# The 1e-9 of the early softmax sums moved from ScalarE to VectorE, with a new order of operations, in a fused attention and gated-MLP kernel

## The chip, the cores and the metric

The kernel runs on one core of one Trainium2 chip. The metric is the time that the device takes for one execution, in microseconds (us). The engines of the core are TensorE (PE in the rows; PEld is its weight load), VectorE (DVE), ScalarE (ACT), GpSimd (POOL) and SyncE (SP), which here only issues DMA transfers. TensorE writes its products into PSUM, which has eight banks of 512 float32 columns; VectorE and ScalarE read them from there.

## What is computed

Causal attention with a bias from cumulative sums, for 8 batches of 8 heads, 576 positions and 64 columns a head, and then a gated MLP on the heads laid side by side:

```python
scores = scale * q @ k.T + min(-(cum[:, None] - cum[None, :]), 0)   # causal
attn = exp(scores - max); attn = attn / (sum(attn) + 1e-09)
x = attn @ v                                  # 8 heads make 512 columns
h = gelu(x @ w_in); u, v = h[..., :512], h[..., 512:]
v_n = (v - mean) / sqrt(var + 1e-06) * g_ln
v_s = w_sg @ v_n + b_sg                       # mixes the 576 positions
out = x + (u * v_s) @ w_out
```

## The kernel before

**Tiles.** A head's 576 rows of scores are cut into five row tiles `it` (64, 128, 128, 128 and 128 rows). For each tile TensorE makes the scores in a bank of the pair `pss` (or, for the 64 rows in the early pass, of `psm`). VectorE adds the mask, writes the tile to `p` and takes the row minimum `mn` (function `ttr`, the `ISA` rows of VectorE: the second of a pair only reads out `mn`). ScalarE takes the exponential with its row sum (`exp_`, sums in `few`). Then `norm` adds 1e-9 to the sums of the head, takes the reciprocal `rs` and multiplies the tiles by it, on an engine that a table names. TensorE transposes the tiles through `psp` (`turned`), an engine copies them to `pT`, TensorE multiplies by `v` (`sums_of`), and two heads together make one tile `xr` of `x`.

**The first batch.** Heads 0 to 7 go in two passes, with operands in full float32: pass a (`scores_a`, `context_a`) makes row tiles 0, 1 and 2, which need only the first 320 keys, and pass b (`scores_b`, `context_b`) makes tiles 3 and 4. The softmax sums of a head in pass a are therefore three columns wide (`rs` 128x3), in pass b two, and from head 8 on five. The buffers of p rotate over three slots (two of `p`, one named `e`). From head 8 on the operands are split into a high and a low part (`kh`, `kl`).

**The MLP.** For each batch there are five v units (xs times the v half of `wi`, then GELU and layer norm on VectorE, ScalarE and GpSimd), eight u units, eight s units (`ws` times `vn`) and eight o units (`wo` times `gt`, added to `xr` and stored). The banks `psm` carry them. The weights `w_in` and `w_out` come in as 64-bit numbers (`pair`) and are turned into two float32 parts with three wide VectorE operations, a ScalarE read and two splitting steps (`wh`, `wl`) for each 128x512 piece. The scratch for that is a bank of `psm`, too.

**Filling work.** 49 matmuls of `wt` into one bank (nine at the start, 40 more in the order) compute nothing that is used. The first v unit writes into that same bank (`psm_63`), so all 49 come ahead of it.

**What sets the order.** Nothing is issued as the code is written. `Plan` collects all 6791 operations with what they depend on. `order` runs a list scheduling with written-out costs (`cost`) and waits (`LAT`) back and forth `ROUNDS` times, and then once more with an offset for every operation from the table `SHIFT`. What comes out is the sequence that every engine gets, and each engine works through its own sequence in order: an instruction that waits holds up all behind it on its engine. The tables `ENG` and `ALT` name, for each kind of step, which engine takes its first, second, third ... occurrence (s ScalarE, g GpSimd, v VectorE): `na` and `nb` are the multiplications by `rs` in the two passes, `ea`, `eb`, `eb1` the copies of transposed tiles, `wh` and `wl` the weight splits, `xva` and `xvb` the copies to `xr`, `xa` and `xal` the splits of `xr`, `n` and `ev` the same for later heads.

```python
res = self.forward(lat, [p + 200.0 * float(x) for p, x in zip(prio, shift)])
...
nc.scalar.activation(out=rs[:, c], in_=sums[pslot(h)][:, c], func=AF.Copy, bias=1e-9)
nc.vector.reciprocal(out=rs[:, c], in_=rs[:, c])
```

Almost all instructions are recorded through one helper, so the rows carry one line number, L441 before (L450 after); they are told apart by the tiles.

Of the kernel before, what the change touches and what calls it, by code (L numbers as in the profile page):

```python
# [23 lines left out]
DH = DFF // 2  # L24
# [45 lines left out]
    "na": "sggggsssgsggsvvsggggvgggsgsgvgvg",  # L70
    "wh": "sssvvggssggg",
    "ea": "ssvsssss",
    "xva": "v",
    "xa": "gvsgsvss",
    "xal": "gv",
    "nb": "gggsvsggggssvggsggv",
    "eb1": "ssvsvsvv",
    "xvb": "ssss",
    "rt": "gvgggv",
    "vl": "gv",  # L80
    "kh": "ssssssssgg",
    "kl": "gggggggvggv",
    "wsh": "sssssssgsvsg",
    "wsl": "gggvgggvgggg",
    "n": "ggggggggggggggggggggggggsggvgsvgggvvvsgsggvvvvsggvsgsgggsv",
    "ev": "svsvssssvsssvssv",
    "ev1": "svsvsvs",
    "xv": "vv",
    "xw": "s",
    "xz": "ss",  # L90
    "gh": "vsvsssv",
    "gl": "vvgggvv",
    "xh": "ss",
# [12 lines left out]
    "c-n2-dHk1C`akf~uAO!jB~g|vS&M90!`KyO>^oz|)-<bO44-JBQfZM&DygJWQM4<iec#ijMSIeEzRz>`&0jzF<K5@|zVEYK%j<ew*E#1_B9sl~{y$ggust"  # L106
    "4#U&giZowzC%3B|+D@#lDr)-hfmdd4TiqhVt_Gkg+jgb-%MD&f2Macma;s^8A|Vptk$hBHHv@b~az{8KnTTpd=$isAR+weU~(?g%%AW}#kq+`ngs7sB;=J"
    "sZ}?E5j3>w+^Qpr%h<5<?G=e`TBi$+4nc{^>TQY9P8p(^WPT!7W&7n@r=+YoD!Z34Z^>|ym&ZP2o1ydI4qV6l|ls)mN#3I&?Qv!yiwR2{~I0&{|)~RSB9V"
    "BzIaR66ibK2ac&$QKZ+gW^7wq%5+}!bF_5^1PlK>Ez8=mZ$#dbs@J)O<d>G$|7aDz1>>IBm-|s@r&^QdyzeB7O7RH5fe|#g{;M>eNFiwcm<2P|kd@WuZ>S"
    "%X3{xv)u&SRG+!@*cTlnQr+=Hb$CVmOWF<KvRJNc+Jt#(LyhA3u%#V^dbDV5VEcpTnypIWBaL{|ejU{o!3wy-Ks!LkT0jqQzaIPwYjm4{7sbtZdZ7v1+*7"  # L110
    "$hE_@Y<IHR`ot4xvLFt~qhA!tg!yFM8cz(@X@5&NAyoFfQ1~_;jAcVrHavkh55;Biig0dt+xJ)5@C~yTgjS(S7#us%_)&IFKEBVrfAa0kX8K(i$oqA}^X~"
    "49Z_?qM@TTXlkonE<UOd9?)8b`(`F3~_*4D-sJUgF`e=|eVa7-Aa#d~BO9;d_}aa8Qi`tP|0#IEsupMmj1S2tGf9zSrWr+>T0-m$H#yB;6LL0S)Sr<-rxJ"
    "na@+#xC()GIw`<s!z9ADU6Ee(zjT+h+UV)S?+zW)y()xe2l%O^Xfd;1U~KpCDlV3VN3kZxSiuy#&|#e5(`7;wD<)7T+7EBMM%GRoWFxa#%2*!AzTuc#dR4"
    "IW1zS-o4qE6USjX_!c=k8gM5ABq<EJ;e-Ia6(lAN-fhRrKV4ya0;^!i(Z(Kvy&&aSXj*KU<{Teci;lmE`3tC^u*S+YplI=c^d&s;w?xoc@mP<DHI&OfolH"
    "n_34ir!QwC+ZqnRMUe{?zzZ_#W~~hnsRlJ`1BeXgf6?Ys{AM9=cWudtmFFupxdDXXA>QBp=S3z1e#RN&Argt@wL-ti=;Au*yG-Q<!c3&E8|&T?1c#G2iXs"
    "kNp3tYbwm09V%-1CbsEF>$z;+fu}ZLm)fBvJ^P97qj5K%G{RVuVY(RnccNuG*XMC1U51L{VeH(AwIk1Mi%01_m6Qwg+#T!E?!2%h?qHQC!-9<Cmtne+Sl_"
    "1Kd&Za(e~Kew7nq;NwtLyS5!PtOLe)Yc^Uf6W?_hzC<AeP8FSczM-sh7+>~N4&=h3)II61t95&DJ$@G&Ajt>x2Zy9EE;6z&hl(&sjOcp^TzM66znwHC$KX"
# [427 lines left out]
def tile_attn_gmlp(  # L545
# [114 lines left out]
    def pslot(h):  # L660
        return h % (3 if h < N3 else 2)
# [789 lines left out]
```

## Time and profile before

| | |
|---|---|
| time, median of two runs | 737.61 us (736.52 and 738.69) |
| the profiled execution | 737.75 us, of which 736.0 us from first to last instruction |
| TensorE busy | 726.3 us, 99% of the span |
| VectorE, ScalarE, GpSimd busy | 483.4, 482.8 and 526.0 us |
| TensorE's granted clock | full speed, mean 0.999 |
| DMA | 88.35 MB, mean 120 GB/s |

A busy share is the time in which an engine has at least one instruction in flight. The shares are means over stages that differ much: the first 120 us build up the pipeline, then follows a long steady part. A row of a timeline gives the start, the time until the last of its instructions ends, engine, operation, and in square brackets how long the engine had been idle before and what ended that.

### The profile page before, as it was taken

How to read it: one execution, taken by the hardware profiler on the slowest of the kernel's cores; microseconds unless marked ns; L12 is line 12 of the kernel's file. 1: busy time of each engine (PE TensorE's matmuls, PEld its weight loads, DVE VectorE, ACT ScalarE, POOL GpSimd, SP SyncE). 2: the span in 40 equal slices, each digit the busy share in tenths (PEclk: the TensorE clock that was granted, in tenths of full speed). 3: DMA queues.
4: the chain of work that ended last, by engine and by line, in shares of the span. 5: the costliest groups of instructions: out<-in, count | busy, mean ns of one | idle time of the engine just before them, and what ended most of it. 6: DMA issues, size and time to landing. Idle time of an engine off the chain costs nothing.

```text
span 736.0 us, 16276 instructions
## 1 busy us (share of the span) xinstructions
PE 726.3 (99%) x5337; PEld 640.8 (87%) x5337; DVE 483.4 (66%) x1524; ACT 482.8 (66%) x1306; POOL 526.0 (71%) x941
## 2 busy tenths in 40 slices
PE   8999999999999999999999999999999999999998
PEld 6876879988899888998889898998889988899998
DVE  6799977777775567646684477746667456844552
ACT  4988986687885667756676568746777457742341
POOL 5775989749779686886858868687775967873532
PEclk9999999999999999999999999999999999999999
DMA  8893744655455443434534444435544354200101
GB/s 210 252 234 102 199 125 121 169 141 149 128 135 133 130 115 104 124 110 124 147 86 119 123 125 127 106 92 144 132 108 119 95 135 114 61 9 34 47 9 64
DMA packets 59272, 88.35 MB, mean 120 GB/s; under 512 B 16306, under 2 KB 33972, under 8 KB 59188
## 3 DMA queue, kind: packets, MB, share of 16 engines
q1 hardware_dynamic: 59188, 87.32, 44.5%
q8 instruction: 42, 0.69, 0.4%
q14 instruction: 42, 0.34, 0.2%
HBM read 41.37 MB, written 9.73 MB: 69 GB/s over the span
## 4 chain that ended last, share of the span: by engine, by line
PE 91%; DVE 3%; DMA 2%; POOL 2%; ACT 1%; issue 1%; SPq 1%; ACTq 0%; DVEq 0%; POOLq 0%
PE psm L441 54%; PE psp L441 21%; PE pss L441 15%; DMA pair<-in_w_in 1%; DVE p L441 1%; SPq L441 1%; DVE psm L441 1%; POOL p L441 0%; DMA raw<-in_kq 0%; POOL wi L441 0%; POOL rt L441 0%; ACT p L441 0%; DVE gt L441 0%; DVE vt L441 0%; DVE u L441 0%
## 5 line engine op out<-in xcount | busy, mean ns | idle before, releaser
L441 POOL TENSOR_SCALAR p<-p,rs 64x64 f32<-64x64 f32 (+4 forms) x396 | 177.8, 458 | 55.9 <-DVE rs L441 37.8
L441 ACT ACTIVATE p<-p,mn 64x64 f32<-64x64 f32 (+4 forms) x310 | 172.5, 558 | 57.4 <-DVE mn L441 55.7
L441 DVE CUSTOM_DVE_ANT_0 p<-pss,mask 128x448 f32<-128x448 f32 (+4 forms) x304 | 121.0, 425 | 37.0 <-PE pss L441 27.7
L441 PE MATMUL psm<-gt,wo 128*128 128x288 f32 x720 | 125.0, 299 | 0.0
L441 PE MATMUL pss<-k,q 128*128 128x288 f32 (+9 forms) x672 | 122.2, 297 | 0.2
L441 PE MATMUL psm<-xs,wi 128*128 128x288 f32 x720 | 119.3, 300 | 0.0
L441 PE MATMUL psm<-ws,vn 128*128 128x288 f32 x708 | 114.1, 297 | 0.0
L441 PEld LDWEIGHTS pss<-k,q 66*128 66x128 f32 (+3 forms) x672 | 102.2, 180 | 9.3 <-DVE mn L441 0.5
L441 POOL TENSOR_TENSOR k<-raw,k 128x576 fp32r<-128x576 f32 x54 | 77.3, 1431 | 44.8 <-ACT k L441 41.1
L441 PE MATMUL psm<-wi,xs 128*128 128x512 f32 (+1 forms) x380 | 106.6, 401 | 1.0 <-DVE gt L441 1.0
L441 PEld LDWEIGHTS psm<-gt,wo 128*128 128x128 f32 x720 | 105.3, 188 | 1.7
L441 PEld LDWEIGHTS psm<-xs,wi 128*128 128x128 f32 x720 | 102.6, 188 | 2.4 <-issue 0.4
L441 PEld LDWEIGHTS psm<-ws,vn 128*128 128x128 f32 x708 | 100.2, 188 | 0.9 <-DVE vt L441 0.3
L441 PE MATMUL psp<-pT,vf 128*64 128x64 f32 (+3 forms) x752 | 90.1, 387 | 0.0
L441 PEld LDWEIGHTS psp<-pT,vf 128*64 128x64 f32 x752 | 46.9, 137 | 43.9 <-issue 32.1
L441 PEld LDWEIGHTS psm<-wi,xs 128*128 128x128 f32 (+1 forms) x380 | 66.3, 184 | 13.2 <-DVE gt L441 1.2
L441 ACT COPY pT<-psp 128x512 f32<-128x512 f32 x130 | 72.0, 581 | 8.7 <-PE psp L441 8.1
L441 PE MATMUL psp<-ident,p 128*128 128x128 f32 x744 | 72.3, 247 | 0.3 <-POOL p L441 0.3
L441 PEld LDWEIGHTS psp<-ident,p 128*128 128x128 f32 x744 | 69.7, 140 | 3.0 <-POOL p L441 0.5
L441 DVE SCALAR_TENSOR_TENSOR u<-u,psm 128x288 f32<-128x288 f32 x120 | 52.7, 445 | 18.6 <-ACT u L441 18.2
L441 POOL TENSOR_TENSOR gt<-u,gt 128x288 fp32r<-128x288 f32 (+1 forms) x62 | 49.6, 804 | 18.7 <-ACT gt L441 18.2
L441 ACT ACTIVATION_READ_ACCUMULATOR p<-p,mn 128x1 f32 (+1 forms) x310 | 58.5, 189 | 0.0
(157 smaller groups left out, 1105.2 us busy)
## 6 DMA issues: line engine op xcount, KB each, us to landing
q<-k SPq DMA_DIRECT2D x168, 144.0 KB
raw<-in_kq SPq DMA_DIRECT2D x56, 288.0 KB
vf<-in_vp SPq DMA_DIRECT2D x56, 192.0 KB
out_t<-u SPq DMA_DIRECT2D x64, 144.0 KB
k<-k SPq DMA_DIRECT2D x56, 144.0 KB
pair<-in_w_in SPq DMA_DIRECT2D x8, 512.0 KB
u<-xs SPq DMA_DIRECT2D x32, 64.0 KB
pair<-in_w_out SPq DMA_DIRECT2D x4, 512.0 KB
```

The lines of the kernel that those rows point to most:

```text
L441: fn(*args, **kw)
```

## The change

There are two parts. In `norm`, for the heads of the first batch (`SPL` is 8) and the call that holds row tile 0, which is the call of pass a, the addition of 1e-9 is a VectorE `tensor_scalar` on 128x3 elements in place of a ScalarE activation. That is eight instructions. Pass b and all later heads keep the ScalarE form.

```diff
     def norm(h, its, rs):
         c = slice(min(its), max(its) + 1)
-        nc.scalar.activation(out=rs[:, c], in_=sums[pslot(h)][:, c], func=AF.Copy, bias=1e-9)
+        if h < SPL and 0 in its:
+            nc.vector.tensor_scalar(out=rs[:, c], in0=sums[pslot(h)][:, c], scalar1=1e-9, scalar2=None, op0=ALU.add)
+        else:
+            nc.scalar.activation(out=rs[:, c], in_=sums[pslot(h)][:, c], func=AF.Copy, bias=1e-9)
         nc.vector.reciprocal(out=rs[:, c], in_=rs[:, c])
```

The other part is the tables. `SHIFT` has new numbers for nearly all operations, in steps of 50 instead of 200, and `ALT` names other engines for some occurrences. Two lines of it as examples:

```diff
-    "na": "sggggsssgsggsvvsggggvgggsgsgvgvg",
+    "na": "sgsgvsgvvvsvsgvsgvgsvgsgsgssssgv",
-    "ea": "ssvsssss",
+    "ea": "ssssvvvs",
-            res = self.forward(lat, [p + 200.0 * float(x) for p, x in zip(prio, shift)])
+            res = self.forward(lat, [p + 50.0 * float(x) for p, x in zip(prio, shift)])
```

The operations and their dependencies are the same; the sequences of the engines change from the first rows to the last. In the late part an instruction moves by some ten places among thousands. In the first 120 us engines change too. Counted in the sequences up to the end of the fifth piece of `w_in` (`gt_133`), VectorE gets in the new kernel the eight additions, two more copies to `pT`, one more copy to `xr` (128x320), four more multiplications by `rs` (128x320, 128x128, two of 64x64) and one more low part of `wi` (128x512). It gives up two casts (`wi` 128x512, `xs` 128x320) and one subtraction (`xs` 128x320). GpSimd has eight multiplications by `rs` and one `wi` part less there, and two `xs` steps more. ScalarE has the eight additions, one multiplication and one copy less, and three multiplications and one cast more.

Three places are shown as they stand in the sequences.

**The start.** SyncE's first transfers before (`in_ka` are the queries and keys of pass a: `kq_80`, `kq_81`, `kq_82` of heads 0, 1, 2, `arena` of the later ones; `in_va` the values):

```order
L441 DMA xs_76<-in_s_t 64x576
L441 DMA kq_80<-in_ka 64x640
L441 DMA kq_82<-in_ka 64x640
L441 DMA pair_105<-in_w_in 128x1024
L441 DMA kq_81<-in_ka 64x640
L441 DMA e_71<-in_va 128x512
L441 DMA pair_121<-in_w_in 128x1024
L441 DMA arena_79<-in_ka 64x1280
L441 DMA pair_112<-in_w_in 128x1024
```

and now:

```order
L450 DMA xs_76<-in_s_t 64x576
L450 DMA kq_80<-in_ka 64x640
L450 DMA pair_105<-in_w_in 128x1024
L450 DMA kq_81<-in_ka 64x640
L450 DMA e_71<-in_va 128x512
L450 DMA pair_121<-in_w_in 128x1024
L450 DMA e_71<-in_va 128x512
L450 DMA kq_82<-in_ka 64x640
L450 DMA pair_112<-in_w_in 128x1024
L450 DMA vf_147<-in_vp 128x320
L450 DMA arena_79<-in_ka 64x1280
```

The keys of head 2 (`kq_82`) moved from the third place to the eighth, those of head 1 from the fifth to the fourth, and those of heads 3 and 4 (`arena`, 64x1280) from the eighth to the eleventh. TensorE's sequence for the same stretch, before (`sel` matmuls add the cumulative sums):

```order
L441 MATMUL psm_63<-wt_77 128x512 x12
L441 MATMUL pss_58<-kq_80 128x320
L441 MATMUL pss_58<-kq_80 128x192
L441 MATMUL psm_63<-wt_77 128x512
L441 MATMUL psm_64<-kq_80 128x64
L441 MATMUL psm_63<-wt_77 128x512 x2
L441 MATMUL pss_59<-kq_81 128x320
L441 MATMUL pss_59<-kq_81 128x192
L441 MATMUL pss_59<-xs_86,sel_88 128x192
L441 MATMUL pss_59<-xs_86,sel_88 128x320
L441 MATMUL psm_64<-xs_86,sel_88 128x64
```

and now:

```order
L450 MATMUL psm_63<-wt_77 128x512 x16
L450 MATMUL pss_59<-kq_81 128x320
L450 MATMUL pss_59<-kq_81 128x192
L450 MATMUL psm_63<-wt_77 128x512
L450 MATMUL pss_58<-kq_80 128x320
L450 MATMUL pss_58<-kq_80 128x192
L450 MATMUL pss_59<-xs_86,sel_88 128x192
L450 MATMUL pss_59<-xs_86,sel_88 128x320
L450 MATMUL psm_64<-kq_80 128x64
L450 MATMUL psm_64<-xs_86,sel_88 128x64
```

Head 1 now comes ahead of head 0, sixteen filling matmuls stand in front of it in place of twelve, and no others between but one. Ahead of the first scores from `arena_79` (head 3) there are 34 filling matmuls now, and 26 before.

**Pass a on VectorE**, around the reciprocals of heads 0 and 1 (`rs_104`, `rs_108`; the `e_71` and `mn_109` rows are the masks of head 2), before:

```order
L441 MEMSET q_0_25_97 2x576
L441 MEMSET vnr_30_102 2x512
L441 RECIPROCAL rs_104<-rs_104 128x3
L441 ISA e_71,mn_109<-pss_58,mask_18_90 128x320
L441 ISA mn_109 128x1
L441 RECIPROCAL rs_108<-rs_108 128x3
L441 ISA e_71,mn_109<-pss_58,mask_89 128x192
L441 ISA mn_109 128x1
L441 TENSOR_SCALAR psm_64<-psm_64 128x512
```

and now:

```order
L450 MEMSET vnr_30_102 2x512
L450 TENSOR_SCALAR rs_104<-few_91 128x3
L450 ISA e_71,mn_109<-pss_58,mask_18_90 128x320
L450 ISA mn_109 128x1
L450 RECIPROCAL rs_104<-rs_104 128x3
L450 ISA e_71,mn_109<-pss_58,mask_89 128x192
L450 ISA mn_109 128x1
L450 TENSOR_SCALAR psm_64<-psm_64 128x512
L450 TENSOR_SCALAR rs_108<-few_91 128x3
L450 SCALAR_TENSOR_TENSOR psm_64<-pair_112,psm_64 128x512
L450 RECIPROCAL rs_108<-rs_108 128x3
```

The additions stand in front of the reciprocals with one other step between, and the step of head 2 that frees the bank `pss_58` comes behind the first of them.

**Pass b, the bank `pss_59` between two heads.** TensorE's sequence before (the 448 columns in the last row but one wait until VectorE has read the 288 columns that the row above them made):

```order
L441 MATMUL psp_60<-ident_87,e_72 128x128 x4
L441 MATMUL pss_58<-arena_79 128x288
L441 MATMUL pss_59<-arena_79 128x288
L441 MATMUL pss_59<-arena_79 128x448
L441 MATMUL psm_63<-xs_125,wi_99 128x288 x3
```

and now:

```order
L450 MATMUL pss_59<-arena_79 128x288
L450 MATMUL psp_62<-ident_87,e_72 128x128 x4
L450 MATMUL psp_60<-ident_87,e_72 128x128 x4
L450 MATMUL pss_58<-arena_79 128x288
L450 MATMUL psm_63<-xs_125,wi_99 128x288 x3
L450 MATMUL psm_63<-xs_131,wi_99 128x288
L450 MATMUL pss_59<-arena_79 128x448
L450 MATMUL psm_63<-xs_131,wi_99 128x288 x2
```

The last 288 columns of the one head come ahead of the transposes, and four matmuls of a u unit stand in front of the 448 columns of the next head. VectorE's sequence at the same place, from the mask of the head before to the step that frees the bank (`mn_162`, `pss_59`), before:

```order
L441 ISA p_68,mn_162<-pss_58,mask_89 128x448
L441 ISA mn_162 128x1
L441 SCALAR_TENSOR_TENSOR vt_152<-psm_64,mv_154,g_b_92 128x512
L441 SCALAR_TENSOR_TENSOR psm_63<-vt_163,psm_63 128x512
L441 SCALAR_TENSOR_TENSOR rt_155<-rt_155 128x1
L441 TENSOR_SCALAR rt_155<-rt_155 128x1
L441 TENSOR_TENSOR rt_155<-rt_155 128x1
L441 BN_STATS bs_164<-psm_63 128x6
L441 TENSOR_SCALAR psm_64<-psm_64 128x512
L441 BN_AGGR mv_165<-bs_164 128x2
L441 ISA p_68,mn_162<-pss_59,mask_18_90 128x288
```

and now:

```order
L450 ISA p_66,mn_159<-pss_59,mask_18_90,mn_159 128x288
L450 ISA mn_159 128x1
L450 SCALAR_TENSOR_TENSOR vt_152<-psm_64,mv_154,g_b_92 128x512
L450 BN_AGGR mv_165<-bs_164 128x2
L450 ISA p_68,mn_162<-pss_58,mask_89 128x448
L450 ISA mn_162 128x1
L450 SCALAR_TENSOR_TENSOR rt_155<-rt_155 128x1
L450 TENSOR_SCALAR rt_155<-rt_155 128x1
L450 TENSOR_TENSOR rt_155<-rt_155 128x1
L450 SCALAR_TENSOR_TENSOR vt_163<-psm_63,mv_165,g_b_92 128x512
L450 ISA p_68,mn_162<-pss_59,mask_18_90 128x288
```

The layer-norm steps of the second v unit (`psm_63`, `bs_164`) went ahead of the 448 columns, and the first step of the next weight piece (`psm_64`, integers) went behind.

## Rows read from the trace of the kernel before

**Rows 1.** The page: busy time by engine, and TensorE's busy tenths in 40 slices.
```profile
PE 726.3 (99%) x5337; PEld 640.8 (87%) x5337; DVE 483.4 (66%) x1524; ACT 482.8 (66%) x1306; POOL 526.0 (71%) x941
...
PE   8999999999999999999999999999999999999998
```

**Rows 2.** The view of stretches: busy us and instructions of each engine, clock, DMA share, GB/s.
```profile
0.00:40.00 40.00, 36.58 (x245) 29.73 (x247) 29.68 (x102) 28.76 (x90) 25.64 (x57) 1.00 0.89 239
9.00:17.00 8.00, 8.00 (x44) 7.01 (x44) 6.13 (x25) 4.55 (x17) 1.32 (x3) 1.00 1.05 244
10.00:40.00 30.00, 29.26 (x221) 23.90 (x221) 23.89 (x88) 25.49 (x86) 17.48 (x34) 1.00 0.93 251
50.00:60.00 10.00, 8.38 (x51) 5.28 (x50) 9.93 (x32) 8.72 (x23) 8.02 (x13) 1.00 0.64 179
200.00:300.00 100.00, 100.00 (x756) 88.67 (x755) 67.00 (x224) 70.33 (x193) 74.72 (x135) 1.00 0.47 122
```

**Rows 3.** The view of waits, TensorE alone: total us, times, longest.
```profile
PE pss L441 <- DMA kq<-in_ka: 1.8, 1, 1.8
PE pss L441 <- DVE mn L441: 1.6, 1, 1.6
PE psm L441 <- DVE gt L441: 1.0, 1, 1.0
...
PE psp L441 <- POOL arena L441: 0.5, 1, 0.5
PE psp L441 <- POOL p L441: 0.3, 1, 0.3
```

**Rows 4.** The view of groups: the filling matmuls (busy us, mean ns, idle before).
```profile
L441 PE MATMUL psm<-wt 128*128 128x512 f32 x49 | 15.0, 436 | 0.9 <-DVE wt L441 0.9
```

**Rows 5.** TensorE's timeline: the scores of heads 1 and 3 begin.
```profile
8.94 1.10 PE L441 MATMUL pss<-kq 128*128 128x320 f32 x4 [1.78 <-DMA kq<-in_ka]
...
14.37 1.06 PE L441 MATMUL pss<-arena 128*128 128x320 f32 x4
```

**Rows 6.** TensorE's timeline where bank `pss_59` is waited for.
```profile
57.03 1.02 PE L441 MATMUL pss<-arena 128*128 128x448 f32 x2 [1.62 <-DVE mn L441]
```

**Rows 7.** VectorE's timeline at the same place.
```profile
55.87 0.68 DVE L441 TENSOR_SCALAR psm<-psm 128x512 int32<-128x512 int32 x1
...
56.55 0.42 DVE L441 CUSTOM_DVE_ANT_0 p<-pss,mask 128x288 f32<-128x288 f32 x1
```

**Rows 8.** The view of groups by form: steps like those that move (mean ns).
```profile
L441 DVE RECIPROCAL rs<-rs 128x3 f32<-128x3 f32 x8 | 1.4, 170 | 0.9 <-ACT rs L441 0.7
L441 DVE MEMSET few<- 128x5 f32 x3 | 0.1, 62 | 0.0
L441 ACT ACTIVATE rs<-few 128x3 f32<-128x3 f32 x8 | 1.5, 196 | 0.0
L441 DVE COPY pT<-psp 128x512 f32<-128x512 f32 x62 | 42.4, 683 | 11.3 <-PE psp L441 11.2
L441 DVE COPY xr<-psp 128x320 f32<-128x320 f32 x1 | 0.5, 492 | 1.6 <-PE psp L441 1.6
L441 DVE TENSOR_SCALAR p<-p,rs 64x64 f32<-64x64 f32 x7 | 2.7, 381 | 0.2
L441 DVE TENSOR_TENSOR k<-raw,k 128x576 fp32r<-128x576 f32 x2 | 1.5, 752 | 0.0
L441 DVE CAST wi<-gt 128x512 fp32r<-128x512 f32 x2 | 0.8, 408 | 0.0
L441 DVE CAST xs<-xr 128x320 fp32r<-128x320 f32 x1 | 0.5, 542 | 0.0
```

**Rows 9.** Timeline: two multiplications by `rs` on VectorE.
```profile
46.13 1.40 DVE L441 TENSOR_SCALAR p<-p,rs 128x512 f32<-128x512 f32 x1
...
60.84 0.44 DVE L441 TENSOR_SCALAR p<-p,rs 128x448 f32<-128x448 f32 x1
```

**Rows 10.** GpSimd's timeline beside the first of those two.
```profile
45.94 1.30 POOL L441 TENSOR_TENSOR wi<-gt,wi 128x512 fp32r<-128x512 f32 x1
```

More of the change, by code (lines that the diff above doesn't have):

```diff
@@ L69 @@
 ALT = {
-    "na": "sggggsssgsggsvvsggggvgggsgsgvgvg",
-    "wh": "sssvvggssggg",
-    "ea": "ssvsssss",
[L73 to L79, printed above, removed]
+    "na": "sgsgvsgvvvsvsgvsgvgsvgsgsgssssgv",
+    "wh": "sssssgvgsggg",
+    "wl": "gggvgvgv",
+    "ea": "ssssvvvs",
+    "xva": "svv",
+    "xa": "ggsggvss",
+    "nb": "gsvggssggssgggsgggv",
+    "eb": "sssvv",
+    "eb1": "ssssssvv",
+    "xvb": "sss",
+    "rt": "gvgvvv",
     "vl": "gv",
-    "kh": "ssssssssgg",
-    "kl": "gggggggvggv",
-    "wsh": "sssssssgsvsg",
+    "kh": "sssssggsg",
+    "kl": "ggggggvgggv",
+    "wsh": "sssssssgsssg",
     "wsl": "gggvgggvgggg",
[L85 to L93, printed above, removed]
+    "n": "gggggsggggvvgsgggsggsgvsgssssvvgsvsssvgvssssvgvgsssvgsggsv",
+    "ev": "sssvsvvvvsvssssv",
+    "ev1": "vsvsss",
+    "xv": "vvv",
+    "xw": "vss",
+    "gh": "sggssssg",
+    "gl": "vgvvvvv",
+    "xh": "vvv",
 }
@@ L110 @@
[L110 to L117, printed above, removed]
@@ new lines @@
+    "#J6{&UnEto^Sw5j3(jV)xj_Zs*sc*Mi<VLrfUGGx<oARhTR<3fFIdgxLPwIWPOYhM=WKa2}d_j`3!0Ny5ZkAt*S*<_M{n&rXzG=I=lijGi(^b1i<n@Vfhd"
+    "aaJcB7pVUKdW53;eb2VE2H$Ro)f$4maz2<N!HV?{ZhWg!SlS;Rkj}csX2e%es3a={wzhR^{KE*yWD$e{+w@<8qO^+x=92F0V?Pzb|oxe8JwMPfJF=?auTj"
+    "N4Z^coLuSuC@;E$6My!faOK2%67%i}J1Mb`J?(E#jQOX0PvR^73>kEL`<vt?f1f3&_=RCNZIgOA+D_Gr^mseP2AtUqa<F;#J}udT4oS7HS-}pF-R&`bHVn"
+    "B&Dlj6i+TZkIJ(eCn7`E(k`Hb7my^$3h?;e)d+(Ujau`TV1DtC~3gFD~vnYi42S6>Z(a!<)0-Q|hv6Hm*NiI2LsCvNud@wfWt?PPX$pnJ*Q0UDfJaGU<{#"
@@ new lines @@
+    "Oo86B#uaY*5;`G5poOfJm|mR?zM_t@9*^&xI<i5B9r*6zrx)v-;qP*a@o+w<h}MOP<d6jSZ~tb)9I#A4yABfSc`6s{t+D&a?z9g|Fx(m`et}r_)d6JI6yv"
+    "ad&`;n6}v*e9My*hqIZPnqL04z?r1oAI65+189g379epy)>D8gn|50y}cS*1-!Uw`PqdUSm(E;H#y+xi41y(j<$J>?mY_y+Tp=X=ZH^{a2LO4g?XnWXj_)"
+    ">VgJ_r)e45!NL-D`4%d|EE2q7S(aS=K4J#4Ss$&-xD6;0EpE@?YAkW%`qmD(>(HyTeY_{jAfzuV2zb?a!euoNIT6YqT+{2^UBAM|+2?zEcjeui4+FP7m{k"
+    "g^h4dIE5LV)ki{BzTyhu-C;wIbH|0hL?6`M{dYB^kGT8oEd6cxuwAde)>Zp}UZ8(4(Fdak!gut3tC369^z-3Xx1sHJz7A@QJ!8+=rE+K3-9IV&`)}JlexB"
@@ new lines @@
+    "L<tvl1cD({gF*(Hz4A^M`fLe6&|m(%Pma=IO3pSCyIae8!kJlfMfAH5vCphxL-`p0m0m~sCpf8(xa(AN*U-}q*Co7*=rU>~&orCH8%`-D^NYA13XbM&zLo"
+    "SbXt%9{KP3~WZvhpTme`&D=*yfgejce&f-aQCo%L@%&s?KV3^50>ADns7JwdPLiG&dv@0!W3Q__R)uJP~RaRwzpa9&bnWczuKPmlK!W>U^zL-2Hl?S44(#"
+    "3H!^$GiAn!gS8^ZnopL>$`@a2?%h|kKBHQ|F*=4WjW%4fjvA!htF%?B>HLtTl^tJGE^horW?&qF&-60dE^n|cqI5|XA<$HFc47gWhKx*|h?UCa_;hc`j{c"
+    "hZ4d|4i`H@T0wC+%PDN{+kR{np;?#^K)A$)k3X-l^ZWoAgk9-u;cqO-q;SaM#MQtm!iUsQZljDpPr}+sE(a4|VT%zmY2cb$74-3vBfb*4bzOA?L_@>;f&w"
@@ L204 @@
+    "P=16gVnQl`>CVs?X&(ugh5GpYTyVT(^X23?Cb#;OMj-AhW(KBiQ^DqNtH{|1|&Shqa+0gz_fL}++wk@n-4lQo?(_pO14bvsA&Lp?Sf2+<Ecf+Oy{Nb7jS#"
+    "cE?S?_14)CTj_fwot%wgt4Nhh4?FZi|(!MrriAJ><bzJFGRQdAhZRJ{GM2M%F_XpI;R!B*_d+TG^S14v=4hy?R6Z_Z_Qv{SIp0$gHlSFw^*zD1I)3N*84-"
+    "{tVp~;-oBDJa(7GiK`yfY{7Hq45lF?wv*1{=bg<=N`Xq3<4?w94Nsh9M;mS!ciZQ>eXIw)zTLMnyCr6~DpBv-5-I%eC=9yc#IJ$#NjHW1Zd3U|_@YzW{Qm"
+    "*qP#b{")
 N3 = 8
```

181 lines of the change are left out of this document (91 added, 90 removed).

## The prediction, made ahead of the run

> **What bounds the kernel now.** I read the page first. TensorE is busy for 726.3 of 736.0 us and its slices show nines from the second to the last but one [rows 1]. In the view of stretches the 100 us from 200 on are full: 100.00 busy for 756 matmuls, one each 0.132 us, while VectorE, ScalarE and GpSimd have a quarter and more of the time free [rows 2]. So TensorE bounds the kernel, the change gives it no matmul more or less, and only the 9.7 us in which it is idle can change hands. A wait of TensorE that goes brings the end forward by its full length, unless the time comes back as another wait. The view of waits names them: 1.8 us for the keys of head 1, 1.6 for VectorE's row minimum, 1.0 for the scratch of a weight piece, 0.5 and 0.3 for tiles that GpSimd multiplies [rows 3]. TensorE starts at 0.9, when VectorE has set `wt` [rows 4], and is not quite full in the last slice [rows 1]. The 49 filling matmuls are busy for 15.0 us [rows 4], and they cost that wherever they stand, since the first v unit comes behind the last of them either way.
>
> The additions themselves reach TensorE only through the softmax of pass a, and VectorE there has room: 29.68 us busy of the first 40, so 10.3 idle, and 23.89 of the 30 from 10 on, so 6.1 idle [rows 2]. Between 50 and 60 it is another matter: VectorE is busy for 9.93 of 10 us and TensorE for 8.38 [rows 2].
>
> **The additions.** Eight ScalarE steps of 0.196 us go (1.6 us), and eight VectorE steps on 128x3 come. The trace has no such step; the reciprocal of the same 128x3 takes 0.170 and a fill of 128x5 takes 0.062 [rows 8]. I take 0.17, the step that also reads and has the same shape: 8 x 0.17 = 1.4 us (0.5 at the lower bound). What they remove is the hand-over: the reciprocals now wait 0.7 us in all for ScalarE's result [rows 8], and in the new order one VectorE step stands between addition and reciprocal, so that nobody waits. Queued behind an addition that waits for the exponential's sum is, for head 0, the mask of head 2, and behind it TensorE's next scores in `pss_58`; the filling matmuls cover that. I cost the additions at nothing; without cover it is 1.4 us, which is in the surplus below.
>
> **What else comes to VectorE up to the fifth weight piece.** Two copies to `pT` at 0.683, a copy to `xr` at 0.492, four multiplications by `rs` between 0.381 (64x64, [rows 8]) and 0.44 (128x448, [rows 9]), together about 1.6, and a low part of `wi`, for which the nearest step takes 0.752 on 576 columns [rows 8], by columns 0.67: 4.1 us. Two casts go, 0.408 and 0.542, and a subtraction, priced like the second of them: 1.5 us. With the additions VectorE has 1.4 + 4.1 - 1.5 = 4.0 us more to do (3.1 with the additions at their lower bound). I cost it at nothing: it lies in the 6.1 us of idle time between 10 and 40. What it costs if that time can't be used is the third rival.
>
> **The start.** The keys of head 2 (64x640 float32, 0.164 MB) no longer come ahead of those of head 1. At 244 GB/s [rows 2] these land 0.67 us sooner than 8.94 [rows 5]. But TensorE also comes to wait sooner: the scores of head 0 from the front (four matmuls; four such take up to 1.10 us, [rows 5], I take 0.7) go behind, and one filling matmul more (15.0 / 49 = 0.31, [rows 4]) comes in front, 0.4 us less work. So the wait of 1.78 [rows 5] shrinks by 0.67 - 0.4: **-0.25 us** (bounds -0.67 and +0.4).
>
> The keys of heads 3 and 4 pay for it. Before, 2.28 MB are moved until they are there (the sizes of the tiles in the sequence, added up), now 3.23 MB. With 1.16 MB landed at 8.94, the other 1.12 MB at 244 GB/s put their arrival at 13.5; TensorE takes them at 14.37 without a wait [rows 5], so 0.9 us were to spare. The 0.95 MB more are 3.9 us: 17.4. TensorE gets there later too, with 34 filling matmuls in front in place of 26: 14.37 - 0.25 + 8 x 0.31 = 16.6. That leaves a wait that the trace of before has not: **+0.8 us** (0 if they came early; 18.3 - 16.6 = 1.7 if they came just in time).
>
> **The bank between two heads.** TensorE waits 1.62 us at 55.4 for VectorE's step on the 288 columns in `pss_59`, which ends near 56.97 [rows 6, 7]. In the new sequence four matmuls of a u unit stand in front of the 448 columns that wait, 4 x 0.132 = **-0.53 us** [rows 2]. VectorE's work up to that step is about as long as before: the layer-norm step of the second v unit and its statistics go ahead, the integer step of 0.68 [rows 7] goes behind. Bounds: -1.62, if the mask then comes in time, and 0, if VectorE is later by the 0.53.
>
> **GpSimd.** It has eight multiplications less up to the fifth weight piece. The two waits of TensorE for tiles that GpSimd made (0.5 and 0.3, [rows 3]) sit in that part: **-0.8 us** (bounds -0.8 and 0, when the tile's new engine is as late).
>
> **The rest.** The steady part keeps its matmuls; for the late order I put 0 and as bounds half the distance of the two runs shown, 1.1 us either way. The end: 0.
>
> **Sum**, on the profiled execution: 737.75 - 0.25 + 0.8 - 0.53 - 0.8 = 737.0. That execution lies 0.14 above the median, so 736.8 for a median. All bounds on one side give 733.4 and 740.8.
>
> **Rivals.** (1) The early part really gets shorter: the waits for the keys, the row minimum and the weight scratch go (1.8 + 1.6 + 1.0) with GpSimd's 0.8 [rows 3], because softmax chains without a ScalarE hand-over put every tile ahead of its need: 737.6 - 5.2 = 732.4. For it: ScalarE and GpSimd get lighter in the same stretch, and these waits have no common cause that must stay. Against it: the first is a transfer, and the second is VectorE's, which gets heavier.
>
> (2) Nothing moves: a wait that goes at one place is paid at the next, since a filling matmul that closes a gap early is missing in a later one: 737.6. For it: the 49 fillers stay 49, and transfers bound the first 17 us (244 GB/s, DMA share 1.05, [rows 2]).
>
> (3) Slower: VectorE's 4.0 us more aren't absorbed. Its idle time before 40 us ends on TensorE's products (11.3 us of the idle time before the copies to `pT` in the whole run, [rows 8]), so idle there is not room that a later step may use. Then all that VectorE does from 40 on, where it is the last to finish, is 4.0 late, and the wait at the bank is 1.62 - 0.53 + 4.0. With the other terms: 736.8 + 4.0 = 740.8. It decides from the point where less than 4.0 of the 6.1 us can be filled.
>
> (4) The steps that come to VectorE are dearer than their rows. At 46.13 a multiplication of 128x512 took 1.40 us on VectorE, with GpSimd's subtraction for `wi` (45.94, 1.30 us) beside it, against 0.44 for 128x448 at 60.84 [rows 9, 10], 0.96 more. Five steps from SBUF to SBUF come (four multiplications and a low part of `wi`); with each of them beside such a step it is 5 x 0.96 = 4.8 us beyond the surplus, and 736.8 + 4.8 = 741.6. The Trainium skill, "SBUF — State Buffer", section "Who interferes with whom", says that VectorE and GpSimd share one pair of ports, which the first to issue holds for its whole instruction, so that the other blocks. By that rule, which speaks against moving such work to VectorE, the trace agrees at this one place (1.40 us). Against the rival: GpSimd has fewer steps there now, and three such steps leave VectorE.
>
> **How the numbers follow.** Forecast 0.40, rival 1 0.20, rival 2 0.16, rival 3 0.14, rival 4 0.10. The likeliest case gives 736.8. The range takes in all centres, 732.4 to 741.6, with half of each outer case's own spread beyond it: 732.0 to 742.0, which leaves out under 2 in 10. A difference of 2%, 14.7 us, is about what a measurement of this kernel can tell from no change; faster by that much would need more than all idle time of TensorE (9.7 us), slower three times the dearest rival's price. So within 2% has 0.95.
>
> **What would show it.** In the profile after: the first scores of head 1 near 8.2 us, with a wait near 1.5; a wait of some 0.8 us for a transfer ahead of the scores of head 3 near 17; the wait at `pss_59` near 1.1; no wait for GpSimd's tiles in the first 40 us; additions of 0.06 to 0.17 us; TensorE's idle time together near 9.0. If VectorE is busy for 9.9 of 10 us well before 50, rival 3 holds. If waits of over 2 us for VectorE stand between 40 and 110, I was wrong about its room; and if the idle time of TensorE shrinks to 5, about what ends those waits.

## The result, and the profile after

The changed kernel takes 746.84 us (two runs, 746.63 and 747.05) against 737.61 us: a ratio of 1.0119, with a 95% interval of 1.0071 to 1.0167. It is slower by 9.2 us, under 2% but clear of noise, and outside the predicted range. The profiled execution took 747.05 us with a span of 745.2. The page after, its busy line, TensorE's busy tenths and its granted clock:

```profile
PE 731.3 (98%) x5337; PEld 643.8 (86%) x5337; DVE 491.3 (66%) x1549; ACT 485.0 (65%) x1307; POOL 515.7 (69%) x914
...
PE   8999989999999999999999999999999999999998
...
PEclk9999989999999999999999999999999999999999
```

The sixth slice of 18.6 us, from 93 us on, is where a digit falls in both rows. TensorE is idle for 745.2 - 731.3 = 13.9 us, 4.2 more than before, and busy for 5.0 us more with the same 5337 matmuls. The view of waits for TensorE after, to be read against [rows 3]:

```profile
PE pss L450 <- DMA k<-k: 3.5, 1, 3.5
PE psm L450 <- DMA vnr<-vnr: 1.3, 1, 1.3
PE pss L450 <- DMA kq<-in_ka: 1.1, 1, 1.1
PE pss L450 <- DVE mn L450: 1.1, 2, 0.7
...
PE psp L450 <- POOL p L450: 0.8, 1, 0.8
PE psm L450 <- DVE gt L450: 0.6, 1, 0.6
PE pss L450 <- DMA k<-cum: 0.5, 1, 0.5
```

The waits that I had priced did shrink, but for GpSimd's (0.8 us in all, as before). What is new is a wait of 3.5 us for `k<-k`, a copy between the two halves of a head's split keys, and one of 1.3 us for the normalised rows. The view of stretches of the changed kernel, the first row to be read against [rows 2]:

```profile
0.00:40.00 40.00, 37.94 (x258) 30.60 (x260) 32.91 (x117) 29.24 (x85) 23.40 (x50) 1.00 0.90 247
60.00:80.00 20.00, 19.38 (x143) 15.72 (x144) 19.54 (x59) 17.95 (x50) 12.08 (x19) 1.00 0.43 133
80.00:100.00 20.00, 16.53 (x113) 13.70 (x111) 19.14 (x53) 16.56 (x48) 16.75 (x25) 1.00 0.60 151
60.00:120.00 60.00, 54.84 (x379) 45.95 (x380) 50.80 (x152) 46.23 (x130) 44.91 (x72) 0.94 0.47 127
120.00:240.00 120.00, 118.70 (x903) 104.32 (x903) 85.68 (x282) 87.36 (x246) 81.90 (x137) 1.00 0.49 131
```

and of the kernel before, from 60 us on:

```profile
60.00:80.00 20.00, 20.00 (x154) 16.74 (x153) 19.32 (x60) 18.93 (x52) 12.78 (x25) 1.00 0.47 133
80.00:100.00 20.00, 18.84 (x130) 16.01 (x131) 18.00 (x53) 17.09 (x49) 17.61 (x30) 1.00 0.64 158
60.00:120.00 60.00, 58.53 (x434) 50.27 (x433) 50.53 (x154) 50.81 (x142) 48.84 (x85) 1.00 0.52 136
120.00:240.00 120.00, 120.00 (x922) 105.14 (x920) 85.64 (x293) 88.43 (x246) 94.75 (x159) 1.00 0.54 143
```

Up to 40 us TensorE is busier than before (37.94 against 36.58 us) although VectorE has 3.2 us more to do. From 60 us on it is the other way round: between 60 and 120 us TensorE does 55 matmuls fewer than before, between 120 and 240 us 19 fewer. At the mean of 0.136 us a matmul (726.3 / 5337) that is about 7.5 and 2.6 us, an estimate, since the matmuls differ in size. From 240 to 600 us both kernels keep TensorE full. So in these two executions nearly all of the loss is made by 240 us, most of it by 120. The place itself, TensorE's timeline and then the stretches around it, after:

```profile
96.46 1.14 PE L450 MATMUL psp<-ident,p 128*128 128x128 f32 x12
101.08 2.31 PE L450 MATMUL pss<-k,q 128*128 128x448 f32 x8 [3.48 <-DMA k<-k]
```

```profile
95.00:100.00 5.00, 2.60 (x19) 2.09 (x18) 4.79 (x11) 2.95 (x10) 2.33 (x4) 1.00 0.73 195
100.00:102.00 2.00, 0.92 (x3) 0.76 (x4) 0.55 (x2) 1.36 (x4) 0.61 (x1) 0.70 0.02 3
102.00:104.00 2.00, 2.00 (x11) 2.00 (x10) 1.90 (x5) 2.00 (x6) 2.00 (x4) 0.50 0.61 139
104.00:106.00 2.00, 2.00 (x10) 1.98 (x9) 1.11 (x7) 0.42 (x2) 1.75 (x7) 0.50 0.90 230
106.00:108.00 2.00, 2.00 (x8) 0.68 (x8) 1.13 (x3) 1.58 (x6) 1.81 (x6) 0.60 0.34 74
108.00:110.00 2.00, 2.00 (x21) 1.20 (x18) 0.94 (x5) 1.71 (x5) 1.66 (x6) 1.00 0.01 2
```

Behind the wait the granted clock (the third number from the end) is 0.50, TensorE's level of 1.2 GHz, until about 107.6 us. It works some 0.9 + 4.0 + 1.6 = 6.5 us at half speed, which loses 3.3. Wait and clock together are 6.8 us, beside a loss of 9.2 in all; part of the 6.8 is paid back, since other waits went. Added up over such rows, TensorE is idle for 2.2 us more than before up to 120 us (1.5 less up to 60, 3.7 more behind) and for 2.1 more between 218 and 618 us, and the low clock costs 3.3. About 1.7 us of longer busy time are left that no row here places. SyncE's timeline ahead of the wait, after and then before:

```profile
89.74 1.80 SPq L450 DMA_DIRECT2D u<-in_w_sgt  x3
91.64 0.55 SPq L450 DMA_DIRECT2D wr<-gt  x1
92.29 1.90 SPq L450 DMA_DIRECT2D q<-k  x2
94.23 0.59 SPq L450 DMA_DIRECT2D u<-in_w_sgt  x1
94.88 0.58 SPq L450 DMA_DIRECT2D vf<-in_vp  x1
95.56 0.46 SPq L450 DMA_DIRECT2D q<-k  x1
96.07 0.58 SPq L450 DMA_DIRECT2D raw<-in_kq  x1
96.76 0.46 SPq L450 DMA_DIRECT2D k<-k  x1
98.18 0.26 SPq L450 DMA_DIRECT2D k<-cum  x1
```

```profile
88.94 1.13 SPq L441 DMA_DIRECT2D q<-k  x2
90.16 1.19 SPq L441 DMA_DIRECT2D u<-in_w_sgt  x2
91.44 0.55 SPq L441 DMA_DIRECT2D q<-k  x1
92.07 1.35 SPq L441 DMA_DIRECT2D wr<-gt  x1
93.53 0.54 SPq L441 DMA_DIRECT2D k<-k  x1
94.12 0.58 SPq L441 DMA_DIRECT2D raw<-in_kq  x1
```

The four copies of one head's split keys and queries (three `q<-k` and `k<-k`) begin at 92.29 instead of 88.94, with two weight pieces, a bias row, a load of values and the next head's raw load put between or ahead of them. Most issues take SyncE 0.46 to 0.60 us, and from 87.5 to 97.2 it is never free. (Followed further back, the profile's chain of that wait leaves SyncE at 95.8 us for steps of GpSimd, which it stays on from 88.9 us; of these steps' order the runs below tested one place.)

### The profile page after: what moved, and what is told of

It is laid out like the page before. It is cut to its first block, busy times and chain, and to the rows that moved or that the text cites. A ratio compares the mean times of both kernels' runs of the same rounds, so it can differ in the third digit from the quotient of the medians.

```text
span 745.2 us, 16263 instructions
## 1 busy us (share of the span) xinstructions
PE 731.3 (98%) x5337; PEld 643.8 (86%) x5337; DVE 491.3 (66%) x1549; ACT 485.0 (65%) x1307; POOL 515.7 (69%) x914
## 4 chain that ended last, share of the span: by engine, by line
PE 86%; DVE 3%; ACT 3%; POOL 3%; DMA 2%; issue 1%; SPq 0%; ACTq 0%; DVEq 0%; POOLq 0%
PE psm L450 51%; PE psp L450 20%; PE pss L450 15%; ACT p L450 1%; POOL p L450 1%; DVE p L450 1%; DMA kq<-in_ka 1%; DMA vnr<-vnr 1%; POOL k L450 1%; DMA k<-k 1%; DMA raw<-in_kq 0%; SPq L450 0%; DVE vt L450 0%; DVE psm L450 0%; ACT u L450 0%
## 5 line engine op out<-in xcount | busy, mean ns | idle before, releaser
L450 POOL TENSOR_SCALAR p<-p,rs 64x64 f32<-64x64 f32 (+4 forms) x377 | 170.1, 461 | 47.3 <-DVE rs L450 27.0
L450 ACT ACTIVATE p<-p,mn 128x448 f32<-128x448 f32 (+4 forms) x310 | 172.5, 559 | 41.4 <-DVE mn L450 39.0
L450 DVE CUSTOM_DVE_ANT_0 p<-pss,mask 64x64 f32<-64x64 f32 (+4 forms) x304 | 121.2, 425 | 34.4 <-PE pss L450 22.0
L450 PE MATMUL pss<-k,q 66*128 66x288 f32 (+9 forms) x672 | 121.7, 299 | 4.5 <-DMA k<-k 3.5
L450 PE MATMUL psm<-gt,wo 128*128 128x288 f32 x720 | 122.5, 299 | 0.0
L450 PE MATMUL psm<-xs,wi 128*128 128x288 f32 x720 | 121.4, 303 | 1.0 <-DVE gt L450 0.6
L450 PE MATMUL psm<-wi,xs 128*128 128x512 f32 (+1 forms) x380 | 109.0, 404 | 0.1
L450 ACT COPY pT<-psp 128x512 f32<-128x512 f32 x126 | 69.5, 582 | 21.1 <-PE psp L450 20.5
L450 POOL TENSOR_TENSOR gt<-u,gt 128x288 fp32r<-128x288 f32 (+1 forms) x60 | 48.1, 807 | 19.0 <-ACT gt L450 18.6
L450 ACT CAST gt<-u 128x288 fp32r<-128x288 f32 (+1 forms) x62 | 26.5, 433 | 52.6 <-DVE u L450 45.4
```

The source lines that it names most:

```text
L450: fn(*args, **kw)
```

## The experiments

The first theory (A) was that SyncE's order costs the time, the second (B) that VectorE's extra work does. In many of these kernels the sequence of all operations is written out as a list, so that engines and order can be exchanged one without the other. Each batch ran beside the kernel before, whose medians were 737.8, 737.7, 738.0, 738.4 and 738.6 us. The changed kernel itself was not run again: its 746.84 stands on two executions, both with a mean clock of 0.995, so a difference of 1 or 2 us from it is not clear of noise. A trace is of one execution, which can lie 3 to 5 us from the median of its kernel.

**Additions, engines and order apart.** Only the eight additions, in the sequences of before:

```diff
-    order = nc.order()
+    order = LIST of the kernel before; norm as changed; ENG and ALT as before
```

> The kernel before, its sequences kept word for word, with only the eight additions taken by VectorE in place of ScalarE. Theory A: the additions are worth nothing either way, 737.6 us within 1 us. Theory B (VectorE has no room): each of the eight delays what stands behind it, up to 1.4 us, 738.5 to 739.5 us.

738.30 us, ratio 0.9999 (0.9984 to 1.0015). The additions are worth nothing. The opposite, the changed kernel with only the additions back on ScalarE:

> The changed kernel with only the eight additions given back to ScalarE, its sequences kept word for word. If the additions are worth nothing, 746.8 us within 1 us; if the hand-over matters in this order, 1 to 2 us slower than 746.8.

745.62 us, 1.2 us under the changed kernel's 746.84, which six runs from 743.7 to 746.8 do not set clearly apart from it. So no price of the hand-over shows; and as the additions cost nothing, this may as well be what more executions of the changed kernel would give. The order of the changed kernel with the engines of before:

> The engines and additions of before, with the sequence of all 6791 operations taken from the changed kernel. Theory A (the order does it): the wait for the key copies near 97 us stays, with the low clock behind it, and the time is 744 to 748 us. Theory B (VectorE's extra work does it, which came with the table of engines): the time is within 2 us of 737.6.

748.43 us (ratio 1.0131), 0.4 above theory A's bounds. TensorE's waits there, the first two rows:

```profile
PE psp L571 <- POOL p L571: 4.6, 5, 1.6
PE pss L571 <- DMA k<-k: 1.7, 1, 1.7
```

The order alone costs as much as the whole change and more, but in part by other waits: made for fewer GpSimd multiplications, it now waits for GpSimd 4.6 us, and 1.7 in place of 3.5 for `k<-k`. The engines of the changed kernel in the order of before:

> The changed kernel's additions and table of engines, with the sequence of all operations taken from the kernel before. The order-only run gave 748.4 us against 746.8 for the whole change and 737.8 for before, so theory A (the order alone costs the time) says: within 2 us of 737.8, a little below it if the engines help as they did there. Theory B (VectorE's extra work has no room): 740 to 742 us, with waits of TensorE for VectorE between 40 and 100 us.

741.89 us (1.0058, 1.0033 to 1.0082), and TensorE's waits:

```profile
PE pss L580 <- DVE mn L580: 3.0, 5, 1.7
PE psm L580 <- DVE mn L580: 1.9, 1, 1.9
PE pss L580 <- DMA kq<-in_ka: 1.3, 1, 1.3
PE psm L580 <- DVE gt L580: 1.3, 1, 1.3
```

Here theory A's expectation failed and theory B's held: the engine table (with the additions, which cost nothing) costs 4.2 us in an order that was not made for it. The trace has waits for VectorE in several places, the longest 1.9 at 20 us and 1.7 at 62.7; it is of the slowest of ten executions, 746.4.

**Where in time.** The sequence of one kernel up to a place and the rest in that of the other:

> The changed kernel for the first 1350 operations of its sequence (about the first 155 us), and from there on the order of before. Theory A1 (the early order costs nearly all): 745 us or more. Theory A2 (the late order has waits of its own, the 1.3 us for a copy of the normalised rows near 214 us and the 0.8 us for a raw load near 605 us): about 743.5 us, 3 us less than the whole change.

743.10 us (1.0070, 1.0049 to 1.0091), near theory A2.

> The kernel before for the first 1350 operations of its sequence, and from there on the order of the changed kernel, engines and additions of before. Theory A1: 738 to 739 us. Theory A2: 740 to 741.5 us, with the waits near 214 and 605 us in it.

741.57 us (1.0039, 1.0013 to 1.0065), theory A2 again. Above 737.7 these are 5.4 and 3.9, together 9.3 of the 9.2 us; by the ratios 5.2 and 2.9. But the junction makes waits of its own: this second kernel's trace has 0.7 us for VectorE's `pT` and 0.6 for `u` between 130 and 153 us, which neither parent has. So has the next one, 1.5 us for `u` at 220 us:

> The kernel before for the first 2000 operations (to about 220 us), from there the changed kernel's order. With the change from 1350 operations on it was 741.6 us. If the late loss is the place near 214 us, it is gone: 738 us within 0.8. If it is spread over the rest, 740 to 741.6 us.

740.80 us (1.0052, 1.0022 to 1.0082), of which the wait at the junction would leave about 1.3 above the kernel before. The traces of the two whole kernels show only one wait more behind 240 us, of 0.8, so the rest may belong to the joint. Cuts earlier on, with the changed engines up to the cut and those of before behind it:

> The changed kernel (engines, additions, order) for the first 497 operations of its sequence, about 60 us, and from there engines and order of the kernel before. The traces had the changed kernel up to 1.4 us ahead at 60 us. If the loss of the early part comes between 60 and 110 us, this is 736 to 738 us; if the first 60 us already carry it (more work for VectorE that comes out later), 740 us or more.

738.62 us (1.0022, 1.0007 to 1.0037), between the two expectations.

> The changed kernel (engines, additions, order) for the first 716 operations of its sequence, about 85 us, and from there engines and order of the kernel before. The cut at 60 us gave 738.6 us, the one at 155 us 743.1 us. Theory A (the loss is made between 85 and 110 us): 738 to 739.5 us. Theory B (VectorE's lateness piles up from 60 us on): 741 us or more.

742.43 us (1.0051, 1.0016 to 1.0086). So the first 60 us cost 1 or 2 us in this form, although the changed kernel's trace is ahead there. That the cut at 85 costs 4 us speaks by itself for theory B, but three of its waits for VectorE (1.1 at 87, 2.1 at 95 and 1.4 at 136 us) are in neither parent's trace at those places, so it settles nothing.

**The chain of key copies.** Six of SyncE's transfers moved at one place (the pairs are operations: the first goes behind the second):

```diff
     order = nc.order()
+    for k, j in ((762, 797), (763, 762), (770, 798), (799, 770), (740, 799), (864, 740)):
+        order.remove(k)
+        order.insert(order.index(j) + 1, k)
```

> The changed kernel (746.84 us) with six of SyncE's transfers put in another order at one place: the copies of the split keys and queries that TensorE waited 3.5 us for (k<-k, issued at 96.76) go ahead of two weight pieces, a bias row, a load of values and the next head's raw load. Theory A (the loss of the early part is SyncE's order, and the low clock behind it follows from that wait): the wait falls from 3.5 to under 1 us, the granted clock stays at full speed, and the time is about 741 us (739.5 to 742.5). Theory B (TensorE's wait is only the place where VectorE's 4.0 us more of work come out): the wait moves to a VectorE or GpSimd tile nearby, and the time stays within 1.5 us of 746.8.

744.66 us, 2.2 less than the changed kernel (five of six executions lie below both of its two, one above): between the two theories. The 3.5 us are gone, but its TensorE timeline has the chain's last and smallest transfer in their place, queued behind the loads:

```profile
98.87 1.56 PE L450 MATMUL pss<-k,q 66*128 66x448 f32 x7 [1.03 <-DMA k<-cum]
```

Only fill the wait, and leave it as long as it is:

```diff
+            if k == 912:
+                o = self.ops[k].calls[0][1][0]
+                for _ in range(16):
+                    self.nc.tensor.matmul(o, self.wt.broadcast_to([P, P]), self.wt.broadcast_to([P, 448]), start=True, stop=True)
```

> The changed kernel with 16 matmuls that compute nothing used (wt into the bank that the waiting scores are about to take) put in front of the scores that wait 3.5 us, and nothing else. If the fall of TensorE's clock to 1.2 GHz (from the wait to about 107.6 us) is brought on by the idle time, the clock now stays at full speed and 6.5 us at half speed come back as about 3.3 us: about 743.5 us (742.5 to 744.5), with the wait itself filled but not shorter. If the clock falls for another reason, the time stays at 746.8 (or 16 matmuls later, at most 750).

744.71 us, and the stretch behind the wait at full clock (the mean over each of six executions is 0.999 or 1.000; it was 0.995 in both of the changed kernel):

```profile
100.00:105.00 5.00, 4.47 (x27) 4.06 (x26) 3.15 (x7) 2.71 (x9) 1.29 (x1) 1.00 0.31 95
```

So the fall of the clock follows from the idle time: with the wait filled it is gone. By the medians, work that computes nothing made the kernel 2.1 us faster; but the six executions go from 742.8 to 746.8, five below both of the changed kernel's and one between them, so how much of the loss the clock is remains the estimate of 3.3 us above. More of the chain mended, first the later place too:

> The changed kernel with SyncE's order mended at the place of e1_sp_head and also near 214 us, where two loads of values now go behind the copy of the normalised rows that TensorE waited 1.3 us for, instead of in front of it. Theory A (SyncE's order at single places costs the time): 1.3 us under e1_sp_head's 744.7, so 743.4 us, without the wait near 214 us. Theory C (the late loss is spread and moves to the next place): 744.7 us within 0.7.

743.70 us, as theory A had it. The later wait, which ended at 220 us (the copy is issued near 214), is gone.

> As e9_sp_both, and the small last transfer of that head's keys (two rows from cum), which TensorE waited 1.0 to 1.2 us for once the other copies came sooner, goes ahead of the load of values and the raw load as well. Theory A (the chain of key copies through SyncE's queue sets the loss at 90 to 110 us): no wait for k<-k or k<-cum over 0.5 us there, full clock in most executions, and 740.5 to 742 us. Theory C (the wait moves on to whatever is next, VectorE's tiles): 743.7 us within 1, with waits for VectorE of 1 us or more near 97 us.

742.83 us, all seven executions below the changed kernel's two, but above theory A's 742: the wait moved on, as theory C has it, though to ScalarE and not to VectorE. No key copy is waited for. The next thing, in TensorE's timeline and then in ScalarE's of this kernel:

```profile
103.95 4.62 PE L450 MATMUL psp<-pT,vf 128*64 128x512 f32 x24 [2.28 <-ACT pT L450]
```

```profile
100.79 0.67 ACT L450 CAST k<-raw 128x576 fp32r<-128x576 f32 x1 [2.41 <-DMA raw<-in_kq]
...
103.34 0.56 ACT L450 COPY pT<-psp 128x512 f32<-128x512 f32 x1
```

ScalarE stands for 2.4 us at the cast of the next head's keys, whose raw load is itself late in SyncE's queue, and the copies that TensorE needs stand behind the cast. Behind this wait the clock falls again (0.72 from 105 to 110 us).

> As e13_cum_first with 8 matmuls that compute nothing used in front of the scores that waited. If the clock still falls in e13_cum_first because of what idle time is left, this keeps it at full speed and is 1 to 2 us faster than e13_cum_first; if the clock no longer falls there, it is up to 1.6 us slower.

742.94 us with full clock in five of six executions: neither better nor worse. It may be that the eight matmuls take what the clock gives; no run parts the two.

**Where the queue's lateness starts.** SyncE waited at 83 us for a GpSimd step, the low part of a head's keys:

```diff
+    for k, j in ((717, 574),):
+        order.remove(k)
+        order.insert(order.index(j) + 1, k)
```

> The changed kernel with one GpSimd step moved: the low part of a head's keys (k from raw) that ran at 83.03 us goes ahead of a low part of w_out (1.28 us), a fill and a part of w_sgt (0.81 us), as it stood before the change; nothing else. SyncE's copy of it, and all that stands behind in SyncE's queue up to the key copies near 95 us, could then be issued about 2 us sooner. If the lateness of that queue starts here, the 3.5 us wait near 97 us falls to 2 us or less, the clock falls less often, and the time is 743 to 745.5 us. If the queue's own order decides, the time stays at 746.8 within 0.8.

745.37 us from 741.5 to 747.6, within the expected bounds, but not by the expected way: the wait for `k<-k` is still there.

```profile
99.92 1.77 PE L450 MATMUL pss<-k,q 128*128 128x448 f32 x8 [3.15 <-DMA k<-k]
```

In its trace SyncE issues the copy of that low part at 84.61, no earlier than in the changed kernel (84.48), since the bias row in front (84.32) now holds the queue.

> That GpSimd step moved, and SyncE's queue mended at both places as in e13_cum_first, but the next head's raw load straight behind the key copies and ahead of the load of values, so that ScalarE's cast of it (with the copies to pT behind it, for which TensorE waited 2.3 us in e13_cum_first) is not held up. If lateness in these two in-order queues is the early loss: 740.5 to 742 us, with no wait over 1.2 us between 85 and 110 us. If the early loss is spread over the engines' loads, it stays at e13_cum_first's 742.8 within 0.7.

742.70 us: the same as without the GpSimd step and the earlier raw load. That is the second expectation, a loss spread over the engines. In its trace, of the slowest of eight executions, TensorE waits 1.2 us for VectorE and 1.4 for ScalarE's copies between 100 and 107 us.

**The other way round, in the kernel before.** The same copies put late, with nothing else changed:

> The kernel before, with one place of SyncE's sequence put as late as in the changed kernel: the copies of the split keys and queries of the head whose scores begin at 96.5 us come behind two weight pieces, and the last of them behind the next head's raw load. Everything else is as before. Theory A (these copies are what TensorE waits for): a wait of 1 to 3 us for k<-k near 96 us and 738.7 to 741 us. Theory B (SyncE's order only shows a lateness that other engines make): 737.7 us within 0.7.

738.24 us, ratio 1.0013 (0.9989 to 1.0036): nothing that can be measured, as theory B said, and no wait for `k<-k` in its trace, which is of the slowest of ten executions. There the last copy is issued at 95.64, and TensorE takes it only at 101.61, 5 us later than before, since two other waits had held it up (2.3 us for a copy of `u`, 2.3 for a weight scratch). So theory A as I put it, that these copies in SyncE's order are the cause by themselves, fails here; that single execution doesn't show what the delay would do to a TensorE on time.

**A long step on VectorE.** In the changed kernel's trace, VectorE's row and GpSimd's beside it:

```profile
94.13 1.68 DVE L450 TENSOR_SCALAR p<-p,rs 64x64 f32<-64x64 f32 x1
```

```profile
93.79 1.30 POOL L450 TENSOR_TENSOR wo<-gt,wo 128x512 fp32r<-128x512 f32 x1
```

A step of 0.381 us elsewhere [rows 8] takes 1.68 beside that subtraction, which ends at 95.09, and the GpSimd multiplication behind it (95.06 to 95.76). Given to ScalarE:

```diff
-    "n": "gggggsggggvvgsgggsggsgvsg...
+    "n": "gggggsggggvsgsgggsggsgvsg...
```

> As e13_cum_first, same sequences, with one 64x64 multiplication taken by ScalarE that took 1.68 us on VectorE at 94.1 us in the changed kernel's trace, beside a GpSimd subtraction of 1.30 us. If that long step (1.3 us over its usual 0.38) is what makes VectorE's next masks and TensorE behind them late, 0.5 to 1.3 us faster than e13_cum_first; if not, the same within 0.5.

744.33 us against 742.83: if anything slower, perhaps because ScalarE was the late engine just there. By the rule of the Trainium skill on shared ports ("SBUF — State Buffer", "Who interferes with whom") a step of VectorE can be held for as long as one of GpSimd runs. The 1.68 us agree in that the step is long just beside two of them; which of them held it the rows do not show. The time does not hang on this step.

## Why the prediction was wrong

**The additions: right.** They cost nothing by measurement (ratio 0.9999). Their size was off: the view of groups after has

```profile
L450 DVE TENSOR_SCALAR rs<-few 128x3 f32<-128x3 f32 x8 | 1.7, 213 | 1.1 <-ACT pT L450 1.1
```

0.213 us each, above the 0.17 that I took for the nearest row.

**VectorE's surplus, absorbed before 40 us: right for that stretch, and the wrong question.** It came as 3.2 us of the predicted 4.0 (32.91 against 29.68), and TensorE waited less in these 40 us, not more; so the dearer steps of rival 4 do not show there either. The room that I did not look at is the one from 60 to 100 us, where VectorE was at 37.3 of 40 before and is at 38.7 now. In the order of before it is not there: the engine table alone costs 4.2 us. That this is near the 4.0 of rival 3 is luck: rival 3 had the whole of it come out as one wait at the bank, and the trace has it in several places with 1.9 as the longest. The new order pays with other waits instead.

**The start: right in place, small in weight.** The scores of head 1 began at 7.90 with a wait of 1.15 (forecast 8.2 and 1.5), and the keys of heads 3 and 4 were waited for 0 us in the changed kernel's trace and up to 1.05 in the others with this start (forecast 0.8). **The bank:** the 448 columns named in the prediction wait no longer (they start at 56.47). But just ahead of them TensorE waits 0.42 us for `vt` in front of the four matmuls of the u unit, and at 60 us 0.73 for the row minimum of the next 288 columns. Together that is 1.15 instead of 1.62, near the forecast of 1.1, but at other places: the size is luck in part. (The other 0.4 of the 1.1 us for `mn` in the view of waits is of another head, at 84.6.) **GpSimd:** the wait of 0.5 us, at 25 us, went as forecast. The one of 0.3 did not sit in the early part, as I had read it, but at 106 us. And 0.8 us come back between 600 and 620 us, so the term is about 0 and not -0.8. **The weight scratch:** 0.6 instead of 1.0.

**The step that failed** is "The rest" and what stood in it: I let 0, with 1.1 us either way, stand for the late order, because the steady part keeps its matmuls. The changed kernel's trace has three things there: 3.7 us more of TensorE's idle time between 60 and 120 us, 3.3 us by the low clock behind the longest wait, and 2.1 us more of idle time between 218 and 618 us. No term of the sum had a transfer that comes late behind 17 us, or the clock. SyncE's sequence is read for its first eleven transfers only, and no place behind 60 us is compared. Busy shares do not show how near to waiting a full engine is. For the keys near 95 us the new order has ScalarE's cast 1.1 us later than before (89.31 for 88.24), GpSimd's low part 1.9 (90.86 for 88.99) and SyncE's last copy 3.2 (96.76 for 93.53), and what comes last sets a wait of 3.5 us that takes the clock down with it. Mending that chain and the later place gives back 4.0 of the 9.2 us (742.83), where the trace had 6.8 and 1.3 us standing there: in its trace TensorE waits for the next engine instead, and the clock falls behind that wait.

**What is shown and what is open.** Shown: the additions cost nothing; the order and the engine table each cost time without the other (10.6 and 4.2 us), so their prices do not add up to the 9.2 of the whole. With SyncE's order mended along that chain and at the later place, 4.0 us come back against the two executions of the changed kernel, so the chain is part of the loss; the single steps on the way, about 2 us each for filling the wait and for the first six transfers, are not clear of noise by themselves. In the traces no mending ends the matter: each wait that was taken away let the next engine's wait through, 2.3 us for ScalarE, then 1.2 and 1.4 for VectorE and ScalarE. Open: why the chain is late in the new order at all, since the same copies put late in the old order cost nothing, and the last 4 to 5 us of the mended versions, nearly all of which the traces of the whole kernels put before 240 us. No version tried beats the kernel before.

## What to carry to other kernels

A new order of all operations is not a sum of the places where it is looked at: for a kernel whose main engine has no idle time, follow each in-order queue, SyncE's first, to the last transfer that the main engine takes, and ask how much later it may come. (No run here tries this as a forecast, and the copies put late in the old order cost nothing, so it tells where to look and not the price.) Engines and order hang together here: either alone cost 4 to 11 us. The eight additions of the title were worth nothing.

## What the runs showed of the hardware that was not expected

A wait of 3.48 us took TensorE's clock from 2.4 to 1.2 GHz for the next 6.5 us of work; waits of 1.78 and 1.62 us in the kernel before left it at full speed [rows 2, 5, 6], and so did one of 2.33 us in the kernel with the additions back on ScalarE (1.00 from 100 to 105 us). By the Trainium skill ("TensorE: Matmul & The Clock Gate", "What's actually happening") the throttled state is the default and activity lifts it; e2_fill_wait agrees, whose unused matmuls kept the clock up. But shorter idle time can do it too: with a wait of 1.03 us near 98 us the clock of the next stretch was 0.72 in one execution.

```profile
100.00:105.00 5.00, 5.00 (x25) 3.69 (x25) 4.48 (x14) 4.55 (x15) 4.39 (x10) 0.72 0.60 150
```

That row is of the kernel with six transfers moved. So the length of one wait does not tell whether the clock falls. The kernel with the key copies put late in the old order shows what such a fall goes with: six executions with a mean clock of 0.999 or 1.000 took 735.8 to 739.1 us, four with 0.995 to 0.997 took 740.1 to 742.2. The difference is not the clock's price alone: the one profiled, 742.2, has a wait of 2.3 us for a copy of `u` ahead of the fall (0.66 from 60 to 65 us).
